# Attention and two routed expert layers on one core: score tiles paired 3 with 0 and 2 with 1, each in a PSUM bank of its own, and three pieces of work moved to other places of the head loop

## The chip, the cores and the metric

The kernel is one program on one core of a Trainium2 chip. The metric is the device time of one execution in microseconds (us). Below, PE is TensorE (PEld its weight loads), DVE is VectorE, ACT is ScalarE, POOL is GpSimd and SP the engine whose queue issues most DMAs.

## The reference

```python
# attention: 4 batches, 12 heads, 448 tokens, head size 64, causal
scores = scale * np.matmul(q, k.transpose(0, 1, 3, 2))
scores = np.where(mask, -1000000000.0, scores)
attn = np.exp(scores - np.max(scores, axis=-1, keepdims=True))
attn = attn / (np.sum(attn, axis=-1, keepdims=True) + 1e-09)
attn_out = np.matmul(attn, v)
x = attn_out.transpose(0, 2, 1, 3).reshape(1792, 768)
# two expert layers, each: every token goes to one of 8 experts
...
    h = np.maximum(x[mask] @ w1[e], 0.0)
    out[mask] = gate_w[mask, None] * (h @ w2[e])
```

The first expert layer adds its result to x and skips tokens whose skip score is not positive; the second uses normalised inner products with expert embeddings as router logits. All arrays are float32.

## The kernel before, in words

The program has two parts. The first, which the change touches, computes attention head by head and, along the way, the logits of both routers. The second part gathers the tokens of each expert and runs the expert layers; nothing of it is changed.

The first part is one loop over 48 heads (`for i in range(n)`, one turn of it is called a **step** here), whose instructions stand in each engine's queue in the order in which the Python code records them. Each engine works its queue off in order, and semaphores hold an instruction until what it needs is done. In step i the kernel does, for head i-1, the **scores** (`scores`, L307): four PE products, one for each block row c of 112 queries, with (c+1)*112 keys, so tiles of 112, 224, 336 and 448 columns for c = 0, 1, 2, 3. The head size is 64, so a product uses only 64 of the array's 128 rows; q and k lie in both halves of the partitions, and two tiles on different halves run at the same time. Then, on DVE, the **stage** (`stage_a`, L318) of each tile adds the mask, scales, and takes the row's extreme, and ACT takes the exponentials (L321). For head i-2 the step also **turns** the 10 blocks of probabilities by PE transposes into three tiles `tp` (`turn`, L331) and copies them out (two copies on DVE, one on ACT, L333).

Work for a pair of heads alternates between even and odd steps. In an **even** step PE multiplies the turned probabilities with the values (`stage_v`, 16 records at L342 into the tile `av`), makes the router products of an earlier pair (`router_pair`, L386, into columns of the tile `bank`; DVE adds them up in `ls`, L391), and ACT copies `av` to `xb` (L347). In an **odd** step PE turns `xb` back (`turn_v`, L353, tile `tv`), DVE divides by the sums and writes the attention output x (`norm_v`, three instructions, L359 to L361), and PE turns the new 128 columns of x for the router (`router_turn`, L373, tile `rt`), which ACT copies to `xs` (L376). `put_x` sends x to DRAM by DMAs from SP.

PSUM has eight banks. Before the change they hold: `s3` (score tile 3), `s20` (score tiles 2 and 0 together), `bank` (score tile 1, the router products `lt` and the logits), `av`, and four banks that are handed round under the tag `tp`. Tiles 2 and 0 use rows 64 to 127 of the array, tiles 3 and 1 rows 0 to 63.

When the logits of a batch are complete, a list of small jobs (`route`) is worked off, one a step: the logits of all tokens (L396 on PE), the choice of expert, the rank of a token within its expert (L460 to L465 on PE, then a chain of small DVE instructions that ends with L168), one-hot tables on POOL, and the entry into the token table (L525 on PE, L528 on DVE). This happens for three batches within the loop; the last batch is done behind it.

Of the kernel before, what the change touches and what calls it, by code (L numbers as in the profile page):

```python
# [7 lines left out]
F32 = mybir.dt.float32  # L8
# [10 lines left out]
B, H, S, D = 4, 12, 448, 64  # L19
CP = 112  # L20
NCH = S // CP
DM = H * D
DF = 1024
NE = 8
NTOK = B * S
P = 128
KC = DM // P
FC = DF // P
CT = 14
NCOL = CT * NE  # L30
# [5 lines left out]
NLG = 17  # L36
# [9 lines left out]
def moe_attention_kernel(tc, qk, vv, w_r, emb, tau, w11, w12, w21, w22, out):  # L46
# [25 lines left out]
    with ExitStack() as top:  # L72
# [148 lines left out]
        with ExitStack() as ctx:  # L221
            ld = ctx.enter_context(tc.tile_pool(name="ld", bufs=2))
            wk = ctx.enter_context(tc.tile_pool(name="wk", bufs=2))
# [32 lines left out]
            ern, en = inv_norm(sm, ess, NE, "en")  # L256

            def embed_squares():
                esq = wk.tile([NE, DM], F32, tag="pt", name="esq")
                nc.scalar.activation(esq, es, AF.Square, accum_out=ess)  # L260

            def embed():
                pe = ps.tile([P, 4 * CP], F32, tag="tp", name="pe", bufs=4)
                for k in range(KC):
                    nc.tensor.transpose(
                        pe[:, k * 8 : k * 8 + 8], es[:, k * P : (k + 1) * P], ident[:NE, :NE])
                nc.vector.tensor_copy(wr[:, :, 8:16], pe[:, 0:48].rearrange("p (k e) -> p k e", e=8))
# [8 lines left out]
                    small.pop(0)()  # L276


            bank = ps.tile([P, 4 * P], F32, tag="s1", name="bank")
            lt, lg_room = bank[:, 2 * CP : 3 * CP], bank[:CP, 3 * CP : 3 * CP + NCH * NLG]  # L280

            def busy_here(n):
                if n:
# [10 lines left out]
            def score_tiles():  # L294
                return dict(
                    st=wk.tile([CP, 10 * CP], F32, tag="st", name="st"),
                    mn=wk.tile([CP, NCH], F32, tag="mn", name="mn"),
                    pr=wk.tile([CP, 10 * CP], F32, tag="pr", name="pr"),
                    s3=ps.tile([CP, S], F32, tag="s3", name="s3"),
                    s20=ps.tile([CP, S], F32, tag="s20", name="s20"),  # L300
                    s1=bank[:CP, 0 : 2 * CP])

            def scores(src, a, c):

                n, r = (c + 1) * CP, 64 * (1 - c % 2)
                a[c] = (a["s20"][:, 3 * CP :], a["s1"], a["s20"][:, 0 : 3 * CP], a["s3"])[c]
                nc.tensor.matmul(a[c], src[r : r + 64, c * CP : (c + 1) * CP], src[r : r + 64, S : S + n],  # L307
                                 start=True, stop=True)

# [14 lines left out]
            def turn_p(pr, pt, i):  # L324

                nb = 4 if i < 2 else 2
                tp = ps.tile([CP, 4 * CP], F32, tag="tp", name="tp", bufs=4)
                for u in range(nb):
                    c, j = BLOCKS[4 * i + u]
                    o = (OFF[c] + j) * CP  # L330
                    nc.tensor.transpose(tp[:, u * CP : (u + 1) * CP], pr[:, o : o + CP], ident[:CP, :CP])  # L331
                dst = pt[:, 4 * i * CP : (4 * i + nb) * CP]
                (nc.scalar.copy if i == 1 else nc.vector.tensor_copy)(dst, tp[:, : nb * CP])  # L333

            def stage_v(g):

                b, hp = divmod(g, H // 2)
                av = ps.tile([P, S], F32, tag="av", name="av")
                for j in range(NCH):
                    o = BLOCKS.index((j, j)) * CP  # L340
                    for u in range(2):
                        nc.tensor.matmul(av[u * D : (u + 1) * D, j * CP :], v_t[b][:, j, 2 * hp + u, :],  # L342
                                         pts[2 * g + u][:, o : o + (NCH - j) * CP],
                                         start=(j == 0), stop=(j == NCH - 1))
                del pts[2 * g], pts[2 * g + 1]
                xb = wk.tile([P, S], F32, tag="xb", name="xb", bufs=1)
                return lambda: nc.scalar.copy(xb, av), xb  # L347

            def turn_v(xb):

                tv = ps.tile([CP, NCH, P], F32, tag="tp", name="tv", bufs=4)
                for t in range(NCH):
                    nc.tensor.transpose(tv[:, t, :], xb[:, t * CP : (t + 1) * CP], ident)  # L353
                return tv

            def norm_v(g, tv):
                b, hp = divmod(g, H // 2)
                rs = sums.pop(g)
                nc.vector.tensor_scalar(rs, rs, 1e-9, None, op0=ALU.add)  # L359
                nc.vector.reciprocal(rs, rs)  # L360
                nc.vector.tensor_tensor(  # L361
                    x_t[b][:, :, hp * P : (hp + 1) * P].rearrange("p t (u d) -> p t u d", u=2),
                    tv.rearrange("p t (u d) -> p t u d", u=2),
                    rs.unsqueeze(3).to_broadcast([CP, NCH, 2, D]), op=ALU.mult)
# [2 lines left out]

                return b == B - 1 and k == KC - 1

            def router_turn(b, k):  # L370
                rt = ps.tile([P, 4 * CP], F32, tag="tp", name="rt", bufs=4)
                for t in range(NCH):
                    nc.tensor.transpose(  # L373
                        rt[:, t * CP : (t + 1) * CP], x_t[b][:, t, k * P : (k + 1) * P], ident[:CP, :CP])
                xs = wk.tile([P, S], F32, tag="xs", name="xs")
                return lambda: nc.scalar.copy(xs, rt), (b, k, xs)  # L376
# [24 lines left out]
            def route(b):  # L401
# [3 lines left out]
                k = {"fill": []}  # L405
# [47 lines left out]

                def rank():
                    oh, some = k["oh"], k["some"]
                    rk = ps.tile([P, 4 * CP], F32, tag="tp", name="rk", bufs=4)
                    wd = NCH * 16
                    o16 = oh.rearrange("p t m e -> p t (m e)")
                    r16 = run[:CP].rearrange("p m e -> p (m e)")
# [60 lines left out]

                def enter(m):
                    roh, voh = k["made"][m]
                    tk = ps.tile([P, NCOL], F32, tag="tp", name="tk", bufs=4)
                    for t in range(NCH):
                        nc.tensor.matmul(tk, roh[:, t, :], voh[:, t, :], start=(t == 0), stop=(t == NCH - 1))  # L525
                    if fast:
                        first_index(0, tk)
                    nc.vector.tensor_tensor(tok[m], tok[m], tk, op=ALU.add)  # L528
                    while k["fill"]:
                        fill()  # L530
# [17 lines left out]
                        lambda: both(enters[0], q1), q2, q3, enters[1]]  # L548

            def turn(i):  # L550
                pts[i] = wk.tile([CP, 10 * CP], F32, tag="pt", name="pt")
                for u in range(3):
                    turn_p(prs[i], pts[i], u)

# [18 lines left out]
            spl, prs, pts, sums = {}, {}, {}, {}  # L573
            with tc.manual_schedule():
                busy_here(12)
                exps = []
                for i in range(n):
                    b, h = heads[i]
                    if h == 0:
# [12 lines left out]
                    if i in EARLY:  # L592
                        early_low(EARLY[i])
                    even = i % 2 == 0
                    if not even and i >= 5:
                        norm_v(i // 2 - 2, turn_v(xb))
                        put_x(i // 2 - 2)
                    if i >= 1:
                        sc = score_tiles()
                        prs[i - 1] = sc["pr"]  # L600
                        for c in (2, 3, 1, 0):
                            scores(spl[i - 1], sc, c)
                        exps = [stage_a(i - 1, sc, c) for c in (2, 3, 1)]
                        exps.pop(0)()
                        little()
                    little()
                    ended = None
                    if even and i >= 4:
                        copy_v, xb = stage_v(i // 2 - 2)
                    add = None  # L610
                    if even and i >= 6:
                        add = router_pair(*pair)
                        ended = pair[0] if pair[1] == KC - 1 else None
                    while exps:
                        exps.pop(0)()
                    if even and i >= 4:
                        copy_v()
                    if i >= 1:
                        stage_a(i - 1, sc, 0)()
                        little()  # L620
                    if add is not None:
                        add()
                    if i == 0:
                        embed_squares()
                    little()
# [2 lines left out]
                    if i >= 2:  # L628
                        turn(i - 2)
                    little()  # L630
                    if not even and i >= 5:
                        copy_x, pair = router_turn(*divmod(i // 2 - 2, H // 2))
                        copy_x()
                    if i == 3:
                        embed()
                    if i + 1 in EARLY:
# [3 lines left out]
                    if ended is not None:  # L640
                        later.extend(route(ended))

                sc = score_tiles()
                prs[n - 1] = sc["pr"]
                for c in (2, 3, 1, 0):
# [7 lines left out]
                    exps.pop(0)()  # L653
                add()
                turn(n - 2)
                norm_v(n // 2 - 2, turn_v(xb))
                later.pop(0)()
                turn(n - 1)
                copy_x, pair = router_turn(B - 1, KC - 2)
                later.pop(0)()  # L660
                copy_x()
                copy_v, xb = stage_v(n // 2 - 1)
# [544 lines left out]
```

## Time and profile before

| | us |
|---|---|
| median of 3 runs | 903.12 (901.76 to 904.38) |
| the profiled execution, its own time | 902.78 |
| its span, first to last instruction | 901.1 |
| PE busy | 824.0 (91%) |
| DVE busy | 554.4 (62%) |
| ACT busy | 474.8 (53%) |
| POOL busy | 135.2 (15%) |

The span is what the profiler shows; the execution's own time is 1.7 us longer. Busy times are sums over the whole program, and its two parts have different limits: the first part takes about the first 230 us of the span.

### The profile page before, as it was taken

What the parts mean: (1) busy time and instruction counts of PE and PEld (TensorE: products, weight loads), DVE (VectorE), ACT (ScalarE), POOL (GpSimd) and SP (SyncE); (2) the same over time, 40 slices, a digit from 0 to 9 for tenths busy, and PEclk for the clock granted to TensorE, in tenths of its full rate; (3) what the DMA queues carried; (4) which work ended last, traced back from release to release, by engine and by line L of the source; (5) the groups of instructions that cost most, each with busy time, mean ns of one, the idle gap of its engine ahead of it and who ended that gap; (6) DMA issues with size and microseconds to landing.
All of it is one profiled execution on the core that took longest, in us unless ns stands there. A gap on an engine that the chain in (4) does not pass through costs nothing. (4 is left out here: it accounts for less than half of the span.)

```text
span 901.1 us, 14898 instructions
## 1 busy us (share of the span) xinstructions
PE 824.0 (91%) x4960; PEld 686.5 (76%) x4960; DVE 554.4 (62%) x1641; ACT 474.8 (53%) x1013; POOL 135.2 (15%) x150
## 2 busy tenths in 40 slices
PE   7998989989797899899999879899999998999994
PEld 5665766666487788788899748789889887889884
DVE  5767767776566688378833476665283268574343
ACT  5777666666455466166612336454272256463252
POOL 1132404013201111011010021011111011110100
PEclk9999999999899899999999999999999999999998
DMA  8979565563636487267710354580451086361000
GB/s 243 315 271 299 165 185 165 167 206 139 202 140 258 175 300 286 72 232 300 299 45 28 145 198 159 197 332 21 149 211 51 19 313 267 133 238 41 37 1 18
DMA packets 59032, 158.22 MB, mean 176 GB/s; under 512 B 13013, under 2 KB 23765, under 8 KB 58448
## 3 DMA queue, kind: packets, MB, share of 16 engines
q1 hardware_dynamic: 52816, 139.33, 43.4%
q0 software_dynamic: 6080, 17.29, 5.4%
q8 instruction: 59, 0.97, 0.5%
q14 instruction: 77, 0.63, 0.2%
HBM read 146.45 MB, written 22.92 MB: 188 GB/s over the span
## 5 line engine op out<-in xcount | busy, mean ns | idle before, releaser
L789 PE MATMUL p<-hi,ht 128*128 128x384 f32 x960 | 241.8, 353 | 8.5 <-DVE ht L773 4.6
L740 DVE TENSOR_TENSOR lo<-raw,hi 128x768 fp32r<-128x768 f32 (+1 forms) x218 | 220.6, 1062 | 8.0 <-ACT hi L736 4.5
L781 PE MATMUL p<-hi,xt 128*128 128x512 f32 x720 | 183.3, 403 | 8.0 <-PEq L1088 3.3
L736 ACT CAST hi<-raw 128x768 fp32r<-128x768 f32 (+1 forms) x218 | 187.3, 923 | 0.6 <-DMA raw<-in_w 0.6
L789 PEld LDWEIGHTS p<-hi,ht 128*128 128x128 f32 x960 | 167.8, 191 | 14.7 <-DVE ht L773 10.6
L781 PEld LDWEIGHTS p<-hi,xt 128*128 128x128 f32 x720 | 140.4, 198 | 37.4 <-ACTq L1088 5.1
L321 ACT ACTIVATE pr<-st,mn 112x336 f32<-112x336 f32 x192 | 99.5, 520 | 60.4 <-DVE mn L318 60.4
L789 PE MATMUL p<-lo,ht 128*128 128x384 f32 x480 | 124.3, 340 | 0.4 <-issue 0.4
L773 DVE SCALAR_TENSOR_TENSOR ht<-tp,ht 128x512 fp32r<-128x512 f32 x60 | 41.4, 689 | 115.3 <-ACT ht L772 106.6
L781 PE MATMUL p<-lo,xt 128*128 128x512 f32 x360 | 96.2, 402 | 0.0
L940 ACT COPY hs<-p 128x512 f32<-128x512 f32 x60 | 34.8, 580 | 106.0 <-PE p L781 67.0
L789 PEld LDWEIGHTS p<-lo,ht 128*128 128x128 f32 x480 | 88.7, 191 | 0.5 <-issue 0.5
L760 ACT CAST xt<-tp 128x384 fp32r<-128x384 f32 (+2 forms) x62 | 30.4, 492 | 109.5 <-PE tp L754 108.8
L761 DVE TENSOR_TENSOR xt<-tp,xt 128x384 fp32r<-128x384 f32 (+2 forms) x62 | 33.3, 544 | 84.5 <-ACT xt L760 81.6
L318 DVE CUSTOM_DVE_ANT_0 st<-s,mask 112x336 f32<-112x336 f32 x144 | 63.5, 465 | 29.4 <-PE s L307 17.8
L781 PEld LDWEIGHTS p<-lo,xt 128*128 128x128 f32 x360 | 67.8, 195 | 11.4
L772 ACT ACTIVATE ht<-tp 128x512 fp32r<-128x512 f32 x60 | 36.0, 600 | 55.1 <-PE tp L798 49.4
L331 PE MATMUL tp<-ident,pr 112*112 112x112 f32 x480 | 57.3, 267 | 0.0
L307 PE MATMUL s<-qk 64*112 64x112 f32 (+2 forms) x288 | 49.6, 450 | 7.1 <-DVE mn L318 7.1
L331 PEld LDWEIGHTS tp<-ident,pr 112*112 112x112 f32 x480 | 47.1, 136 | 8.6 <-issue 7.8
L818 POOL DMA_INDIRECT out<-py,pidx x18 | 19.7, 1093 | 207.7 <-ACT hi L736 75.5
L342 PE MATMUL av<-pt,v 112*64 112x448 f32 (+3 forms) x384 | 50.6, 405 | 0.0
(201 smaller groups left out, 908.3 us busy)
## 6 DMA issues: line engine op xcount, KB each, us to landing
raw<-in_w SPq DMA_DIRECT2D x96, 512.0 KB
raw<-in_w SPq DMA_DIRECT2D x128, 384.0 KB
qk<-in_qk SPq DMA_DIRECT2D x23, 896.0 KB
x<-x SPq DMA_DIRECT2D x24, 448.0 KB
v<-in_vv SPq DMA_DIRECT2D x4, 1344.0 KB
qk<-in_qk SPq DMA_DIRECT2D x2, 448.0 KB
g_n<-x,L POOLq DMA_INDIRECT x23, 4.4
out<-py,pidx POOLq DMA_INDIRECT x18, 3.4
```

What stands on the lines that cost most here:

```text
L307: nc.tensor.matmul(a[c], src[r : r + 64, c * CP : (c + 1) * CP], src[r : r + 64, S : S + n], start=True, stop=True)
L318: nc.vector.tensor_tensor_reduce(out=so, in0=a[c], in1=mask[:, S - n : S], scale=-0.125, scalar=3.0e38, op0=ALU.add, op1=ALU.min, accum_ou ...
L321: return lambda: nc.scalar.activation(a["pr"][:, OFF[c] * CP : OFF[c] * CP + n], so, AF.Exp, bias=mn, scale=-1.0, accum_out=rs)
L331: nc.tensor.transpose(tp[:, u * CP : (u + 1) * CP], pr[:, o : o + CP], ident[:CP, :CP])
L342: nc.tensor.matmul(av[u * D : (u + 1) * D, j * CP :], v_t[b][:, j, 2 * hp + u, :], pts[2 * g + u][:, o : o + (NCH - j) * CP], start=(j == ...
L736: copy(hi, raw)
L740: eng.tensor_tensor(lo, raw, hi.bitcast(F32), op=ALU.subtract)
L772: nc.scalar.activation(hi, src, AF.Relu)
L773: nc.vector.scalar_tensor_tensor(lo, src, 0.0, hi.bitcast(F32), op0=ALU.max, op1=ALU.subtract)
L781: nc.tensor.matmul(p1[u], xt[:, k, :, j], r[:, u * 512 : (u + 1) * 512], start=(k == 0 and j == 0 and not low), stop=(k == KC - 1 and low))
L789: mm = nc.tensor.matmul(p2[u], l, r[:, u * (DM // 2) : (u + 1) * (DM // 2)], start=(f == 0 and j == 0), stop=(f == FC - 1 and j == len(ter ...
L940: nc.scalar.copy(hs[:, u * 512 : (u + 1) * 512], p1[u])
```

## The change

The four score tiles get a bank each. Tile 0 moves into `bank`, beside `lt` and the logits; tiles 1, 2 and 3 have tiles of their own. Tiles 3 and 0 use array rows 0 to 63, tiles 2 and 1 rows 64 to 127. The stages of all four tiles are now recorded together. `tp` has three banks in place of four. `av`, `tv` and `rt` share one bank under the tag `av`. In an even step `router_turn` (of the pair before) moves to the head of the step, ahead of the scores, and `router_pair` and then `stage_v` to its end, behind the turn of head i-2. In an odd step the copy of `av` and the addition to `ls` stand first, then the scores and the four stages, and then `turn_v` and `norm_v`, which stood ahead of the scores before. The turned probabilities `pt` have three buffers in place of two. Behind the loop, the last steps follow the same order and use the tag `tp` where the change gives one.

```diff
             def scores(src, a, c):
-                n, r = (c + 1) * CP, 64 * (1 - c % 2)
-                a[c] = (a["s20"][:, 3 * CP :], a["s1"], a["s20"][:, 0 : 3 * CP], a["s3"])[c]
+                n, r = (c + 1) * CP, (0, 64, 64, 0)[c]
+                a[c] = (a["s0"], a["s1"], a["s2"], a["s3"])[c]
...
-                av = ps.tile([P, S], F32, tag="av", name="av")
+                av = turned_room("av")[:, 0:S]
...
+            def turned_room(tag):
+                return ps.tile([P, 4 * P], F32, tag=tag, name="turned", bufs=3 if tag == "tp" else 1)
...
-                    if not even and i >= 5:
-                        norm_v(i // 2 - 2, turn_v(xb))
-                        put_x(i // 2 - 2)
+                    if even and i >= 6:
+                        copy_x, pair = router_turn(*divmod(i // 2 - 3, H // 2))
+                        copy_x()
+                    if not even and i >= 5:
+                        copy_v()
+                        if add is not None:
+                            add()
                     if i >= 1:
...
-                        exps = [stage_a(i - 1, sc, c) for c in (2, 3, 1)]
-                        exps.pop(0)()
+                        exps = [stage_a(i - 1, sc, c) for c in (2, 3, 1, 0)]
                         little()
                     little()
-                    ended = None
-                    if even and i >= 4:
-                        copy_v, xb = stage_v(i // 2 - 2)
-                    add = None
-                    if even and i >= 6:
-                        add = router_pair(*pair)
-                        ended = pair[0] if pair[1] == KC - 1 else None
+                    if not even and i >= 5:
+                        norm_v(i // 2 - 2, turn_v(xb))
+                        put_x(i // 2 - 2)
                     while exps:
                         exps.pop(0)()
-                    if even and i >= 4:
-                        copy_v()
                     if i >= 1:
-                        stage_a(i - 1, sc, 0)()
                         little()
-                    if add is not None:
-                        add()
...
                     if i >= 2:
                         turn(i - 2)
                     little()
-                    if not even and i >= 5:
-                        copy_x, pair = router_turn(*divmod(i // 2 - 2, H // 2))
-                        copy_x()
+                    ended, add = None, None
+                    if even and i >= 6:
+                        add = router_pair(*pair)
+                        ended = pair[0] if pair[1] == KC - 1 else None
+                    if even and i >= 4:
+                        copy_v, xb = stage_v(i // 2 - 2)
```

What stands in the queues shows the moves better. The first place is PE in an odd step and the head of the even step behind it; `s_` with a number is a score tile, `turned` the shared bank. Before:

```order
L353 MATMUL tv<-ident,xb 112x128 x4
L307 MATMUL s_499<-qk_330 112x336
L307 MATMUL s_498<-qk_330 112x448
L307 MATMUL bank<-qk_330 112x224
L307 MATMUL s_499<-qk_330 112x112
L331 MATMUL tp<-ident,pr 112x112 x10
L373 MATMUL rt<-ident,x_123 128x112 x4
L307 MATMUL s_546<-qk_330 112x336
```

and with the change:

```order
L308 MATMUL s_495<-qk_333 112x336
L308 MATMUL s_494<-qk_333 112x448
L308 MATMUL s_496<-qk_333 112x224
L308 MATMUL bank<-qk_333 112x112
L358 MATMUL turned<-ident,xb 112x128 x4
L332 MATMUL tp<-ident,pr 112x112 x10
L378 MATMUL turned<-ident,x_123 128x112 x4
L308 MATMUL s_553<-qk_333 112x336
```

The transposes of `xb` (L353, now L358) moved behind the scores of their step; those for the router (L373, now L378) still stand between the odd step's turn and the even step's scores, but they now turn the columns of x which the odd step itself has just made.

The second place is DVE in the same odd step, with the semaphores that each instruction waits for; ISA is the stage of a score tile. Before:

```order
L359 TENSOR_SCALAR rs<-rs 112x8
L360 RECIPROCAL rs<-rs 112x8 [waits DVE_49]
L361 TENSOR_TENSOR x_123<-tv,rs 112x4x128 [waits DVE_49,PE_49]
L318 ISA st,mn<-s_605,mask 112x336 [waits PE_49,Activation_49]
L318 ISA mn 112x1
L318 ISA st,mn<-s_604,mask 112x448
...
L318 ISA st,mn<-bank,mask 112x224
...
L318 ISA st,mn<-s_605,mask 112x112
...
L333 COPY pt<-tp 112x448 [waits PE_49,Activation_49]
```

and with the change:

```order
L319 ISA st,mn<-s_605,mask 112x336 [waits PE_49,Activation_49]
L319 ISA mn 112x1
L319 ISA st,mn<-s_604,mask 112x448 [waits PE_49]
...
L319 ISA st,mn<-s_606,mask 112x224 [waits PE_49]
...
L319 ISA st,mn<-bank,mask 112x112 [waits PE_49]
...
L364 TENSOR_SCALAR rs<-rs 112x8
L365 RECIPROCAL rs<-rs 112x8 [waits DVE_49]
L366 TENSOR_TENSOR x_123<-turned,rs 112x4x128 [waits DVE_49,PE_49]
L334 COPY pt<-tp 112x448 [waits PE_49]
```

The three instructions of `norm_v` moved from ahead of the four stages to behind them. Before, only the first stage waits for PE; with the change each stage has a wait of its own.

The third place is PE in an even step, behind its scores. Before:

```order
L342 MATMUL av<-pt,v_121 64x448 x2
...
L342 MATMUL av<-pt,v_121 64x112 x2
L386 MATMUL bank<-xs,wr 32x112 x4
L331 MATMUL tp<-ident,pr 112x112 x10
L353 MATMUL tv<-ident,xb 112x128 x4
```

and with the change:

```order
L332 MATMUL tp<-ident,pr 112x112 x10
L391 MATMUL bank<-xs,wr 32x112 x4
L343 MATMUL turned<-pt,v_121 64x448 x2
...
L343 MATMUL turned<-pt,v_121 64x112 x2
```

The turn moved ahead, and the router's products and then the values' products come last; the router's products write the tile `bank`, in which score tile 0 of the same step now lies. The order of SP's DMAs is the same in both kernels.

## Rows read from the trace of the kernel before

**Rows 1.** Busy time by stretch: length, busy us (instructions) by engine, PE clock, DMA share, GB/s:

```profile
21.45:215.38 193.94, 179.98 (x1488) 126.94 (x1488) 141.82 (x585) 135.26 (x433) 45.59 (x54) 0.98 0.68 221
```

**Rows 2.** Timeline of PE, odd and even step: start, us, line, operation (idle in brackets):

```profile
203.81 1.01 PE L307 MATMUL s<-qk 64*112 64x336 f32 x6
204.66 0.54 PE L307 MATMUL bank<-qk 64*112 64x224 f32 x2
205.13 1.17 PE L331 MATMUL tp<-ident,pr 112*112 112x112 f32 x10
206.14 0.55 PE L373 MATMUL rt<-ident,x 112*128 112x112 f32 x4
206.99 1.01 PE L307 MATMUL s<-qk 64*112 64x336 f32 x6 [0.30 <-DVE mn L318]
...
208.31 2.11 PE L342 MATMUL av<-pt,v 112*64 112x448 f32 x16
210.34 0.40 PE L386 MATMUL bank<-xs,wr 128*32 128x112 f32 x8
210.67 1.17 PE L331 MATMUL tp<-ident,pr 112*112 112x112 f32 x10
211.68 0.60 PE L353 MATMUL tv<-ident,xb 128*112 128x128 f32 x4
212.21 0.63 PE L307 MATMUL s<-qk 64*112 64x336 f32 x2
```

**Rows 3.** Timeline of PE, narrow windows: through tile 2's last pass; tile 1's first pass:

```profile
206.99 0.81 PE L307 MATMUL s<-qk 64*112 64x336 f32 x3 [0.30 <-DVE mn L318]
...
207.84 0.35 PE L307 MATMUL bank<-qk 64*112 64x224 f32 x1
```

**Rows 4.** Timeline of DVE in the odd step of rows 2:

```profile
203.81 0.16 DVE L359 TENSOR_SCALAR rs<-rs 112x8 f32<-112x8 f32 x1
...
204.30 0.69 DVE L361 TENSOR_TENSOR x<-tv,rs 112x512 f32<-112x512 f32 x1
205.37 0.51 DVE L318 CUSTOM_DVE_ANT_0 st<-s,mask 112x336 f32<-112x336 f32 x1 [0.37 <-PE s L307]
...
206.85 0.08 DVE L318 DVE_READ_ACCUMULATOR2_ANT mn<- 112x1 f32 x1
206.85 0.92 DVE L333 COPY pt<-tp 112x448 f32<-112x448 f32 x2
```

**Rows 5.** Timeline of ACT in the same step:

```profile
205.92 0.57 ACT L321 ACTIVATE pr<-st,mn 112x336 f32<-112x336 f32 x1 [2.04 <-DVE mn L318]
...
207.98 0.51 ACT L333 COPY pt<-tp 112x448 f32<-112x448 f32 x1
```

**Rows 6.** Timeline of PE and DVE in two steps with router jobs:

```profile
76.74 0.41 PE L396 MATMUL bank<-ident,ls 128*112 128x68 f32 x2 [1.59 <-DVE mn L318]
76.99 1.12 PE L331 MATMUL tp<-ident,pr 112*112 112x112 f32 x10
...
87.98 0.16 DVE L484 TENSOR_SCALAR base<-bm 112x8 f32<-112x8 f32 x1
...
88.84 0.16 DVE L168 TENSOR_TENSOR lp_o<-base,lp_c 112x8 f32<-112x8 f32 x1
```

**Rows 7.** Timeline of PE in the first steps:

```profile
9.10 1.01 PE L307 MATMUL s<-qk 64*112 64x336 f32 x6 [2.04 <-DVE mn L318]
...
15.95 0.50 PE L265 MATMUL pe<-ident,x 8*128 8x8 f32 x6 [1.05 <-issue]
```

**Rows 8.** PE's waits by line, 21.45 to 215.38 us: total, times, longest:

```profile
PE bank L396 <- DVE mn L318: 4.8, 3, 1.6
...
PE rt L373 <- DVE rks L476: 2.7, 3, 0.9
```

**Rows 9.** Busy time in two stretches of that part; the clock is third from the end:

```profile
131.40:134.80 3.40, 3.40 (x16) 2.74 (x15) 1.92 (x9) 1.57 (x6) 0.00 (x0) 0.50 0.21 60
186.00:189.40 3.40, 3.40 (x18) 3.12 (x20) 1.92 (x11) 2.00 (x8) 0.00 (x0) 0.50 0.02 5
```

More of the change, by code (lines that the diff above doesn't have):

```diff
@@ L258, in embed_squares @@
             def embed_squares():
-                esq = wk.tile([NE, DM], F32, tag="pt", name="esq")
+                esq = wk.tile([NE, DM], F32, tag="pt", name="esq", bufs=3)
                 nc.scalar.activation(esq, es, AF.Square, accum_out=ess)
             def embed():
-                pe = ps.tile([P, 4 * CP], F32, tag="tp", name="pe", bufs=4)
+                pe = ps.tile([P, 4 * CP], F32, tag="tp", name="pe", bufs=3)
                 for k in range(KC):
@@ L276, in little @@
                     small.pop(0)()
-            bank = ps.tile([P, 4 * P], F32, tag="s1", name="bank")
-            lt, lg_room = bank[:, 2 * CP : 3 * CP], bank[:CP, 3 * CP : 3 * CP + NCH * NLG]
+            bank = ps.tile([P, 4 * P], F32, tag="s0", name="bank")
+            lt, lg_room = bank[:, CP : 2 * CP], bank[:CP, 2 * CP : 2 * CP + NCH * NLG]
             def busy_here(n):
@@ L299, in score_tiles @@
                     s3=ps.tile([CP, S], F32, tag="s3", name="s3"),
-                    s20=ps.tile([CP, S], F32, tag="s20", name="s20"),
-                    s1=bank[:CP, 0 : 2 * CP])
+                    s2=ps.tile([CP, 3 * CP], F32, tag="s2", name="s2"),
+                    s1=ps.tile([CP, 2 * CP], F32, tag="s1", name="s1"),
+                    s0=bank[:CP, 0:CP])
             def scores(src, a, c):
-                n, r = (c + 1) * CP, 64 * (1 - c % 2)
-                a[c] = (a["s20"][:, 3 * CP :], a["s1"], a["s20"][:, 0 : 3 * CP], a["s3"])[c]
+                n, r = (c + 1) * CP, (0, 64, 64, 0)[c]
+                a[c] = (a["s0"], a["s1"], a["s2"], a["s3"])[c]
                 nc.tensor.matmul(a[c], src[r : r + 64, c * CP : (c + 1) * CP], src[r : r + 64, S : S + n],
@@ L326, in turn_p @@
                 nb = 4 if i < 2 else 2
-                tp = ps.tile([CP, 4 * CP], F32, tag="tp", name="tp", bufs=4)
+                tp = ps.tile([CP, 4 * CP], F32, tag="tp", name="tp", bufs=3)
                 for u in range(nb):
@@ L347, in stage_v, with turn_v @@
                 return lambda: nc.scalar.copy(xb, av), xb
-            def turn_v(xb):
-                tv = ps.tile([CP, NCH, P], F32, tag="tp", name="tv", bufs=4)
+            def turned_room(tag):
+                return ps.tile([P, 4 * P], F32, tag=tag, name="turned", bufs=3 if tag == "tp" else 1)
+            def turn_v(xb, tag="av"):
+                tv = turned_room(tag)[:CP].rearrange("p (t n) -> p t n", t=NCH)
                 for t in range(NCH):
@@ L368, in direct, with router_turn @@
                 return b == B - 1 and k == KC - 1
-            def router_turn(b, k):
-                rt = ps.tile([P, 4 * CP], F32, tag="tp", name="rt", bufs=4)
+            def router_turn(b, k, tag="av"):
+                rt = turned_room(tag)[:, 0 : 4 * CP]
                 for t in range(NCH):
@@ L455, in rank @@
                     oh, some = k["oh"], k["some"]
-                    rk = ps.tile([P, 4 * CP], F32, tag="tp", name="rk", bufs=4)
+                    rk = ps.tile([P, 4 * CP], F32, tag="tp", name="rk", bufs=3)
                     wd = NCH * 16
@@ L522, in enter @@
                     roh, voh = k["made"][m]
-                    tk = ps.tile([P, NCOL], F32, tag="tp", name="tk", bufs=4)
+                    tk = ps.tile([P, NCOL], F32, tag="tp", name="tk", bufs=3)
                     for t in range(NCH):
@@ L550, in turn @@
             def turn(i):
-                pts[i] = wk.tile([CP, 10 * CP], F32, tag="pt", name="pt")
+                pts[i] = wk.tile([CP, 10 * CP], F32, tag="pt", name="pt", bufs=3)
                 for u in range(3):
@@ L575, in moe_attention_kernel @@
                 busy_here(12)
-                exps = []
+                exps, add = [], None
                 for i in range(n):
@@ L641, in moe_attention_kernel @@
                         later.extend(route(ended))
+                copy_x, pair = router_turn(B - 1, KC - 3, "tp")
+                copy_x()
                 sc = score_tiles()
@@ L655, in moe_attention_kernel @@
                 turn(n - 2)
-                norm_v(n // 2 - 2, turn_v(xb))
+                norm_v(n // 2 - 2, turn_v(xb, "tp"))
                 later.pop(0)()
                 turn(n - 1)
-                copy_x, pair = router_turn(B - 1, KC - 2)
+                copy_x, pair = router_turn(B - 1, KC - 2, "tp")
                 later.pop(0)()
```

## The prediction

> **What bounds the kernel now.** I read the busy time by stretch first, then the timelines of PE, DVE and ACT over one pair of steps, then PE's list of waits. Between 21.45 and 215.38 us lies the loop from step 5 to the scores of the last head: 21 pairs of an odd and an even step, and step 47. PE is busy there for 179.98 of 193.94 us, DVE for 141.82 [rows 1]. So PE looks like the bound, but that is an average over two kinds of step.
>
> An ordinary pair lasts 8.40 us (203.81 to 212.21) [rows 2]. The even step, 206.99 to 212.21, is 5.22 us and PE does not wait in it: scores 1.32, values 2.03, router products 0.33, turn 1.01, transposes of `xb` 0.53. The odd step is 3.18 us and ends with a wait: PE stands 0.30 before the next scores until DVE has read the last score tile. Its length is DVE's: from the start of the scores 1.56 us until the first stage starts (203.81 to 205.37), 1.56 for the four stages (205.37 to the end of the last read at 206.93), 0.06 until PE goes on [rows 2, 4]. `norm_v` costs nothing now: DVE runs it (203.81 to 204.99) while PE still makes the scores.
>
> **The change, part by part.**
>
> *Halves of the rows.* Before, one half of the array carries 448 + 224 columns, the other 336 + 112; with the change both carry 560. The longer half loses 112 columns. The second pass over tile 1's 224 columns adds 0.54 - 0.35 = 0.19 us [rows 2, 3], so two passes of 112 are 0.19, and the block falls from 1.32 to 1.13. That is 0.19 in each step, if PE is what the step waits for.
>
> *A bank and a signal for each tile.* The first stage now waits for tile 2 alone. Tile 2's last pass ends 0.81 after the scores start [rows 3]; before, the first stage started 0.17 after the end of the last product (204.66 + 0.54 = 205.20, to 205.37) [rows 2, 4]. So it starts at 0.98 in place of 1.56, 0.58 earlier. Lower bound 0.90, if a single wait is quicker; upper bound 1.56, if DVE in effect still waits for all four, against which stands that each stage has its own wait. Tile 3 follows without a gap: all passes of the `s` tiles are over 1.01 after the start, 0.2 behind tile 2 [rows 2, 3], and tile 2's stage lasts 0.51 [rows 4]. I take 0.98.
>
> *Odd step.* Now the order on DVE is four stages, then `norm_v`; and the router's transposes at the next head need the x which this `norm_v` writes. The chain is: first stage at 0.98; the instruction behind the stages starts 1.48 later (205.37 to 206.85); `norm_v` takes 1.18 (203.81 to 204.99); PE goes on 0.06 later, at 3.70 [rows 4]. PE itself is ready earlier: scores 1.13, transposes of `xb` 0.53, turn 1.01, so at 2.67. **A new wait of 1.03 us**, ahead of the transposes for the router; behind it in PE's queue stand the next head's scores, so everything waits. The transposes take 0.55 (0.85 to the next scores, less the 0.30) [rows 2]. The odd step is 3.70 + 0.55 = 4.25, against 3.18.
>
> *Even step.* Scores 1.13 and turn 1.01: PE reaches the router's products at 2.14. They write `bank`, where tile 0 of the same step lies, and must wait for its stage: 0.98 + 1.56 + 0.06 = 2.60. A second wait, 0.46. Then router products 0.33 and values 2.03: 4.96, against 5.22. Why a wait is due between different columns of one tile shows in the row on the logits: they too lie in `bank` beside a score tile, and PE stood 1.59 us there until DVE had read it [rows 6]. The Trainium skill, "PSUM — Partial Sum Buffer", section "PSUM bank collisions raise a hardware error", wants PSUM guarded by bank and not by address; the row agrees. By addresses alone the even step would be 0.46 shorter.
>
> *Sum for a pair:* 4.25 + 4.96 = **9.21 against 8.40**. The 0.19 of the halves is in neither chain: both go from the start of the scores to tile 2 and then through DVE. The Trainium skill, "TensorEngine Tiling (Array Packing)", section "PSUM Bottleneck", warns that tiling speeds up TensorE and not the emptying of PSUM; that speaks against this edit, and rows 4 agree, with 1.56 us of stages behind a block of 1.32.
>
> *What is hidden.* The copy of `av` (0.51, ACT, like its copy in [rows 5]) at the odd step's head runs during the scores; without that cover it would add 0.5. Exponentials start 0.55 after the first stage and their copy ends 2.57 after they start [rows 4, 5], so at about 4.1 in the odd step; the next turn comes at 4.25 + 1.13. The two copies of `pt` (0.92) and the addition to `ls` follow on DVE during the wait-free values' products. The third `pt` buffer and three `tp` banks in place of four cost nothing in an ordinary pair, since a turn uses three. `put_x`'s DMAs issue some 2.5 us later in the step; behind them on SP stand the next q, k and weights, which are needed steps later.
>
> *Router jobs.* They make some steps of a batch longer in both kernels. With the change, per batch: the logits wait for tile 0's stage until 2.60, cost 0.25 [rows 6], and the turn of 1.01 ends at 3.86 against 3.70: +0.16. The choice of expert is about 1 us of small DVE work behind the copies, which delays the next first stage by about 0.2. In the rank step the third `tp` waits for ACT's copy at 4.1: +0.65; the chain behind it, 1.02 (87.98 to 89.00) [rows 6], delays the next first stage by 0.3. The two entries into the token table hold the third `tp` until DVE has added: +0.4 each. Together 2.1 a batch; of the third batch only the first 1.3 fall in this part: 5.5.
>
> *Sum.* 21 x 9.21 + 4.25 + 5.5 = 203.2, against 193.94: **+9.2**. *First steps:* the second head's scores no longer wait 2.04 [rows 7], since tile 2's bank is free after its own stage; the turn behind it is then set by the exponentials, 1.1 earlier; the embeddings' wait of 1.05 shrinks a little, and step 4 has no `xb` to turn: together I estimate -2.3 (between -3.5 and -0.5). *Last steps:* three `tp` banks for more users, +0.5 (0 to 1.5). *Clock:* PE ran at half its clock, 1.2 in place of 2.4 GHz, for two stretches of 3.4 us, each soon after a wait of 1.59 [rows 6, 8, 9]; a third such wait and all of 0.9 had none. A stretch at half costs at most half its length, about 1.6. The waits of 1.59 are gone, those of 1.03 are many, one a batch is about 1.4. The 193.94 holds two such stretches, my 203.2 holds none; I add one, +1.6 (0 to 5).
>
> 9.2 - 2.3 + 0.5 + 1.6 = +9.0. The profiled execution took 902.78, 1.7 more than its span; that gives 911.8. The median of the runs is 0.34 above it: **912 us**. The second part is unchanged and starts later by as much.
>
> **The rivals.**
>
> *Faster, because the router's transposes do not wait.* If x were ready when PE has turned, the odd step would end at 2.67 + 0.55 and the pair be 8.18: 22 x 1.03 less, 889 us. If the even step's wait went too, 879. For it: DVE is idle for over a quarter of the part [rows 1]. Against it: the four stages and `norm_v` are one after the other on one engine, with measured lengths. It decides when a pair comes out 0.4 shorter than 9.21, 0.2 in each step's way through DVE.
>
> *No difference.* A pair near 8.8, which the start of the first stage at 0.90 and shorter latencies would nearly give, or a larger gain at the beginning: 901 to 905.
>
> *Slower still by the clock.* PE now idles 1.5 us in every pair. Should some six more stretches run at half, the time is about 922; ten, 928. For it: two waits of 1.59 were followed by such a stretch [rows 6, 9]. Against it: waits of 0.9 were not. The Trainium skill, "TensorE: Matmul & The Clock Gate", section "HAM oscillation — how this bites in real kernels", tells of kernels that lose clock through idle spells between groups of products; no ordinary pair shows it here.
>
> *Slower still by the signals.* If the first stage still starts at 1.56, both steps are 0.58 longer: 21 x 1.16 more, 936.
>
> **How the numbers follow.** My forecast has 0.72, with 907 to 918 as its own range (0.1 a pair either way is 2 us, the beginning and the clock the rest). The clock has 0.10, the signals 0.03, no difference 0.07, faster 0.08. About 0.3% (2.7 us) is what a measurement of this kernel can tell from no change. Slower is thus 0.85, the same 0.07, faster 0.08. The range that leaves out no more than 2 in 10 is 904 to 921.
>
> **What would show it.** Right: PE idle about 1 us ahead of the router's transposes in nearly every even step, released by DVE's instruction that writes x; about 0.45 ahead of the router's products, released by the read of `mn`; a pair of 9.2 us; first stages about 1.0 after the scores start; a score block of 1.13. Wrong: transposes for the router without a wait, first stages at 1.5, a pair under 8.6, or granted clock well under 0.98 in this part.

## The result and the profile after

The changed kernel takes 915.02 us (median of 4 runs, 913.47 to 917.46), the kernel before 903.15 in the same comparison (901.76 to 904.38): ratio 1.0136, 95% interval 1.0114 to 1.0158. The forecast was 912, range 904 to 921, slower. The profiled execution took 914.93, its span is 913.2. The top of its page:

```profile
span 913.2 us, 14795 instructions
PE 819.6 (90%) x4960; PEld 685.6 (75%) x4960; DVE 550.3 (60%) x1641; ACT 476.7 (52%) x1013; POOL 138.3 (15%) x150
```

Busy time by stretch: the first steps, the stretch from step 5 to the last head's scores that answers to [rows 1], and the one half-clock stretch ahead of it (length, busy us by engine, PE clock third from the end):

```profile
4.80:22.62 17.82, 12.89 (x86) 9.38 (x85) 12.05 (x60) 10.76 (x37) 0.00 (x0) 0.90 0.88 242
22.62:226.58 203.96, 172.54 (x1493) 125.79 (x1492) 138.21 (x587) 139.19 (x439) 45.64 (x54) 1.00 0.66 208
17.40:20.80 3.40, 3.40 (x19) 2.69 (x17) 2.47 (x10) 2.39 (x9) 0.00 (x0) 0.50 0.49 154
```

The loop is 10.02 us longer than in [rows 1] although PE is busy 7.44 less: PE waits more. The first steps end 1.17 later (22.62 against 21.45). What follows the last head's scores takes 913.2 - 226.58 = 686.6 against 901.1 - 215.38 = 685.7. So 10.0 of the 12.1 us of span lie in the loop. PE's list of waits there (us in total, times, longest) names two new ones:

```profile
PE turned L378 <- DVE x L366: 12.9, 13, 1.3
PE bank L391 <- DVE mn L319: 6.3, 16, 0.6
```

Together they are 19.2 of the 31.4 us for which PE is idle in the loop; before, it was idle there for 14.0.

The timeline of PE over an ordinary pair (odd step from 212.61, even step from 216.87) answers to [rows 2]:

```profile
212.61 1.19 PE L308 MATMUL s<-qk 64*112 64x336 f32 x6
213.46 0.35 PE L308 MATMUL bank<-qk 64*112 64x112 f32 x2
213.75 0.65 PE L358 MATMUL turned<-ident,xb 128*112 128x128 f32 x4
214.23 1.12 PE L332 MATMUL tp<-ident,pr 112*112 112x112 f32 x10
216.33 0.60 PE L378 MATMUL turned<-ident,x 112*128 112x112 f32 x4 [0.98 <-DVE x L366]
216.87 1.19 PE L308 MATMUL s<-qk 64*112 64x336 f32 x6
...
218.00 1.17 PE L332 MATMUL tp<-ident,pr 112*112 112x112 f32 x10
219.54 0.40 PE L391 MATMUL bank<-xs,wr 128*32 128x112 f32 x8 [0.37 <-DVE mn L319]
219.87 2.11 PE L343 MATMUL turned<-pt,v 112*64 112x448 f32 x16
221.91 0.63 PE L308 MATMUL s<-qk 64*112 64x336 f32 x2
```

The pair is 9.30 long (most are 4.24 + 5.04 = 9.28), 8.40 before. Its two brackets are the two new waits: 0.98 ahead of the router's transposes, ended by the instruction of `norm_v` that writes x, and 0.37 ahead of the router's products, ended by the read of `mn` behind tile 0's stage. DVE in the same pair answers to [rows 4]:

```profile
213.58 0.51 DVE L319 CUSTOM_DVE_ANT_0 st<-s,mask 112x336 f32<-112x336 f32 x1 [2.47 <-PE s L308]
...
215.06 0.20 DVE L364 TENSOR_SCALAR rs<-rs 112x8 f32<-112x8 f32 x1
215.29 0.20 DVE L365 RECIPROCAL rs<-rs 112x8 f32<-112x8 f32 x1
215.59 0.69 DVE L366 TENSOR_TENSOR x<-turned,rs 112x512 f32<-112x512 f32 x1
216.19 0.91 DVE L334 COPY pt<-tp 112x448 f32<-112x448 f32 x2
217.83 0.51 DVE L319 CUSTOM_DVE_ANT_0 st<-s,mask 112x336 f32<-112x336 f32 x1 [0.73 <-PE s L308]
...
219.31 0.08 DVE L319 DVE_READ_ACCUMULATOR2_ANT mn<- 112x1 f32 x1
```

DVE stands idle for 2.47 us until tile 2 is there, works through the stages and `norm_v` with pauses of 0.1 at most, and PE waits for the end of just that chain. Neither engine is full; each waits for the other in turn.

By its ordinary pairs the loop would have lost more: 21 times 0.88 and 1.06 for the last odd step are 19.5. Steps with the router's jobs gave 9.5 of that back: over and above ordinary steps they and the two half-clock stretches [rows 9] took 14.4 before and 4.8 with the change, where the jobs fall into time in which PE waits anyway.

PE in the first steps answers to [rows 7]:

```profile
6.68 1.55 PE L308 MATMUL s<-qk 64*112 64x336 f32 x6 [0.48 <-DVE mn L319]
...
12.21 1.17 PE L308 MATMUL s<-qk 64*112 64x336 f32 x6 [2.10 <-DMA qk<-in_qk]
...
16.31 0.53 PE L265 MATMUL pe<-ident,x 8*128 8x8 f32 x6 [1.80 <-ACT pt L334]
...
18.37 2.11 PE L332 MATMUL tp<-ident,pr 112*112 112x112 f32 x10
```

The last line lies in the half-clock stretch: ten transposes take 2.11 there, 1.12 to 1.17 in the pair above.

### The profile page after: what moved, and what is told of

Read it like the earlier page. It is cut to its first block, busy times and chain, and to the rows that moved or that the text cites. A ratio compares the mean times of both kernels' runs of the same rounds, so it can differ in the third digit from the quotient of the medians.

```text
span 913.2 us, 14795 instructions
## 1 busy us (share of the span) xinstructions
PE 819.6 (90%) x4960; PEld 685.6 (75%) x4960; DVE 550.3 (60%) x1641; ACT 476.7 (52%) x1013; POOL 138.3 (15%) x150
## 5 line engine op out<-in xcount | busy, mean ns | idle before, releaser
L785 PE MATMUL p<-hi,xt 128*128 128x512 f32 x720 | 184.0, 404 | 10.5 <-PEq L1092 3.9
L319 DVE CUSTOM_DVE_ANT_0 st<-s,mask 112x336 f32<-112x336 f32 x144 | 65.5, 504 | 66.8 <-PE s L308 66.0
L308 PE MATMUL s<-qk 64*112 64x448 f32 (+2 forms) x288 | 58.1, 476 | 2.6 <-DMA qk<-in_qk 2.1
L343 PE MATMUL turned<-pt,v 112*64 112x448 f32 (+3 forms) x384 | 50.7, 406 | 0.0
```

The costliest lines, as they stand in the source:

```text
L319: nc.vector.tensor_tensor_reduce(out=so, in0=a[c], in1=mask[:, S - n : S], scale=-0.125, scalar=3.0e38, op0=ALU.add, op1=ALU.min, accum_ou ...
L785: nc.tensor.matmul(p1[u], xt[:, k, :, j], r[:, u * 512 : (u + 1) * 512], start=(k == 0 and j == 0 and not low), stop=(k == KC - 1 and low))
```

## The experiments

The theory under test was the prediction's: an ordinary pair pays for two waits of PE on DVE's chain, one made by the place of the router's transposes, one by the place of the router's products. Rivals were a loss by the clock, a loss by the new tiles and banks themselves, and a gain from the halves that something else eats. All kernels compute the same as the kernel before; no work is left out.

**1. Router's transposes behind the scores** (place alone; everything else as changed):

```diff
-                    if even and i >= 6:
-                        copy_x, pair = router_turn(*divmod(i // 2 - 3, H // 2))
-                        copy_x()
...
                         for c in (2, 3, 1, 0):
                             scores(spl[i - 1], sc, c)
+                        if even and i >= 6:
+                            copy_x, pair = router_turn(*divmod(i // 2 - 3, H // 2))
+                            copy_x()
```

> Theory (two waits in a row of PE behind DVE): with the router's transposes behind the even step's scores, x is written (3.7 us after the odd step's scores began) before PE comes to them, so the wait of 1.0 us ahead of them goes. The wait ahead of the router's products stays or grows, since DVE, still busy with the odd step, now begins the even step's stages late (about 4.5 us after the odd step's scores began): a pair of about 8.5 in place of 9.28, about 899 us. Rival (the time went with the shared bank of the turned tiles and the third tp bank, not with the order): both stay, so 913 to 917.

Measured: 902.26 (10 runs), ratio 1.0008 (0.9985 to 1.003), 3 above the 899 expected. The odd step falls from 4.24 to 2.67, the pair to 8.46. PE's list of waits over the loop (total, times, longest) shows where part of the gain stays:

```profile
PE bank L391 <- DVE mn L319: 6.3, 10, 0.8
...
PE bank L391 <- ACT pr L322: 3.6, 5, 0.7
```

Of the wait for x at L378 one of 0.2 is left, and the one ahead of the router's products has grown. DVE comes late to the even step: in the pair at 201.61 it is still at the odd step's copies when the even step's scores start (204.28), the first stage starts 1.74 later (0.96 in the changed kernel), and PE waits 0.75 for the read of tile 0.

**2. Values ahead of the router's products** at the end of the even step:

```diff
                     ended, add = None, None
+                    if even and i >= 4:
+                        copy_v, xb = stage_v(i // 2 - 2)
                     if even and i >= 6:
                         add = router_pair(*pair)
                         ended = pair[0] if pair[1] == KC - 1 else None
-                    if even and i >= 4:
-                        copy_v, xb = stage_v(i // 2 - 2)
```

> Theory: with the values' products ahead of the router's products, tile 0's stage is over before PE comes to the tile bank, and the wait of 0.4 to 0.5 us in each even step goes; the wait of the odd step stays. Pair about 8.77, about 904 us. Rival (only the wait at the router's transposes sets the pace, and what is saved here is waited for there): 913 to 917.

Measured: 903.66 (10 runs), ratio 1.0021 (1.0001 to 1.0042). The pair is 4.23 + 4.60 = 8.83. The wait ahead of the transposes stays, the other is covered by the values' products:

```profile
205.20 0.61 PE L378 MATMUL turned<-ident,x 112*128 112x112 f32 x4 [0.94 <-DVE x L366]
205.74 1.19 PE L308 MATMUL s<-qk 64*112 64x336 f32 x6
...
207.97 2.11 PE L343 MATMUL turned<-pt,v 112*64 112x448 f32 x16
210.01 0.40 PE L391 MATMUL bank<-xs,wr 128*32 128x112 f32 x8
```

**3. Both moves.**

> Both moves together. Theory: neither wait is left in an ordinary pair and PE's own products set it, 7.6 to 7.7 us; about 882 us, and in any case well under the kernel before. Rival (DVE's or ACT's load, not the place of the waits, keeps the pair from going under that of before): 900 or more.

Measured: 889.73 (4 runs, 885.75 to 897.01), ratio 0.9876 (0.9811 to 0.994): faster than the kernel before, but 8 above the 882 expected. The pair came out as foreseen, 2.67 + 4.99 = 7.66, as long as PE's work:

```profile
189.21 1.19 PE L308 MATMUL s<-qk 64*112 64x336 f32 x6
190.06 0.35 PE L308 MATMUL bank<-qk 64*112 64x112 f32 x2
190.34 0.65 PE L358 MATMUL turned<-ident,xb 128*112 128x128 f32 x4
190.83 1.12 PE L332 MATMUL tp<-ident,pr 112*112 112x112 f32 x10
191.88 1.19 PE L308 MATMUL s<-qk 64*112 64x336 f32 x6
...
193.01 0.60 PE L378 MATMUL turned<-ident,x 112*128 112x112 f32 x4
193.45 1.12 PE L332 MATMUL tp<-ident,pr 112*112 112x112 f32 x10
194.50 2.11 PE L343 MATMUL turned<-pt,v 112*64 112x448 f32 x16
196.54 0.40 PE L391 MATMUL bank<-xs,wr 128*32 128x112 f32 x8
196.87 1.20 PE L308 MATMUL s<-qk 64*112 64x336 f32 x6
```

No bracket is left. The loss of the change was thus made by two places in the queue, and not by its tiles and banks. What was not foreseen are the steps with the router's jobs: the loop takes 181.65 (19.89 to 201.54), 18.1 more than ordinary steps alone, where the changed kernel had 4.8. PE still waits 12.1 us in it, most of them at jobs, and these now lengthen the loop.

**4. The new tiles, halves and banks in the order of before** (shared bank for `av`, `tv`, `rt`; three `tp`, the four stages recorded together; the moves undone).

> The kernel before in its own order, with the change's score tiles, halves and banks (three tp banks, one bank for the three turned tiles), and the four stages recorded together. Theory (what an order costs is its waits, and the banks alone don't shorten the way round): the odd step is short, about 2.7, since the next scores wait only for tile 2's bank, but the values' products now wait about 1 us for ACT's copy of the router's transposes out of the shared bank; a pair of about 8.7 against 8.40, 905 to 912 us. Rival (the new halves and banks are a gain by themselves, and only the moves lose it): a pair of 7.7 to 8.0, under 895.

Measured: 893.0 (4 runs, 892.2 to 893.97), ratio 0.9889 (0.9855 to 0.9922): the expectation of 905 to 912 missed. The pair came out as foreseen, 2.62 + 6.0 = 8.62, with the wait that the shared bank makes:

```profile
205.81 2.11 PE L343 MATMUL turned<-pt,v 112*64 112x448 f32 x16 [0.87 <-ACT xs L377]
```

But the steps with router jobs were cheaper than worked out (even ones 5.04, without that wait), so from the first scores to the last head's the attention took 206.8 against 209.8. Some 2.0 of that was lost again between the loop and the expert layers. And the expert layers, whose code nothing here touches, took 650.4 from their first transposes to the end of the span, against 658.1. Experiments 9 to 11 ask why.

**5 and 6. The old halves** in the changed kernel, and in the kernel with both moves:

```diff
-                n, r = (c + 1) * CP, (0, 64, 64, 0)[c]
+                n, r = (c + 1) * CP, 64 * (1 - c % 2)
```

> The changed kernel with tiles 3 and 1 on one half of the rows and 2 and 0 on the other, as before; banks and order stay changed. Theory (the 0.19 us of a shorter score block lie in front of a wait, so they are worth nothing): 914 to 917, with the block at 1.32 and the waits shorter by 0.19 each. Rival (the halves pay in each of 48 steps): 924.

> The kernel with both moves (e3, pair 7.66) and the old halves, tiles 3 and 1 on one half. Theory (the halves pay where no wait stands behind the score block): both steps 0.19 longer, a pair of 8.04, about 8 us slower than e3, near 898. Rival (they pay nowhere, something else sets e3's pair): pair still 7.66, 890.

Measured in the changed kernel: 918.43 (912.38 to 920.84), ratio 1.0192 (1.0152 to 1.0233), a little above the 914 to 917 expected, and the times don't tell it from the change. The steps do: 4.23 + 5.04, the same, and the loop 203.99 for 203.96. PE's scores take longer and its waits are shorter by as much, 10.5 in 13 times ahead of L378 in place of 12.9. With both moves the same edit costs 0.19 in each step, 2.86 + 5.18 against 2.67 + 4.99, and 897.22 (8 runs, ratio 0.9946, 0.9923 to 0.997). The halves are worth what was counted for them, once no wait stands behind them.

**7 and 8. The embeddings' transposes in the shared bank** in place of the third `tp`, in the changed kernel and with both moves:

```diff
-                pe = ps.tile([P, 4 * CP], F32, tag="tp", name="pe", bufs=3)
+                pe = ps.tile([P, 4 * P], F32, tag="av", name="turned")
```

> The changed kernel with the embeddings' transposes in the bank of the turned tiles, which is free then, in place of a tp bank. Theory (of the 1.80 us wait in the first steps about 1.0 is for the third tp bank, the rest for the scaled embeddings): the wait falls to about 0.8 and is released by DVE's scaling. Rival (it waits for the embeddings anyway, as the kernel before did for 1.05): it stays above 1.5. The time of one run tells nothing at this size.

> Both moves and the embeddings' transposes in the turned tiles' bank: the candidate that should beat both kernels. Theory: e3's time less 0 to 2 us, 886 to 890, about 1.5% faster than before. Rival: no better than e3, or within 0.3% of before.

In the changed kernel (912.14, one run) the wait falls from 1.80 to 0.87 and is ended by another instruction:

```profile
14.80 0.53 PE L265 MATMUL turned<-ident,x 8*128 8x8 f32 x6 [0.87 <-DVE x L271]
```

With both moves it is 1.14, ended by the same instruction. What that is worth in time is not shown: step 5's scores start at 20.32 and 20.34, and at 19.89 to 22.62 in the five profiles of kernels with the first steps of the changed one (table below). With both moves the time is 891.35 (6 runs, ratio 0.9848, 0.9809 to 0.9888), not to be told from experiment 3, where 886 to 890 was expected.

**9 to 11. ACT's waits without a releaser.** In the expert layers of the kernel before, ACT stands twice for 5 to 6 us where the profile names nothing it waits for ("issue"):

```profile
278.79 0.58 ACT L940 COPY hs<-p 128x512 f32<-128x512 f32 x1 [5.91 <-issue]
...
304.63 0.48 ACT L835 COPY yt<-tp 128x384 f32<-128x384 f32 x1 [4.86 <-issue]
```

Ahead of the first, the instruction that waits for PE's product ended at 273.65; the copy behind it began at 278.79. PE waits for the second one (`pm` <- `yt`, 3.2 us), and a half-clock stretch of 6.8 us begins at 305.47. (A third such line, 4.1 us ahead of L835 at 521.22, is in every kernel; there the transposes that it copies began only at 520.59.) The changed kernel and experiments 1 to 3 and 5 to 8 have such a pair at another place of the program, the same one in all of them (424.27 and 449.55 in the changed kernel, 4.23 and 5.58). Experiment 4 has neither. The three groups differ in how many instructions the trace records on ACT: 1432, 1408 and 1454. The work is the same; the number of instructions that only wait for a semaphore differs. So small copies that nobody reads were added on ACT, which is idle for 30% of the loop [rows 1]:

```diff
+                    if 8 <= i < 30:
+                        nc.scalar.copy(dz, ident[:NE, 0:1])
```

This is one copy a step, 22 in all; for 46 it is two a step in steps 8 to 30. The ratios in the table are to the kernel before as measured beside each.

> The kernel before with 22 copies of 8 numbers on ACT, one a step in steps 8 to 29, that nobody reads; nothing else is changed. It asks where the 7.7 us come from that the kernel with the new tiles in the old order won behind the attention, where its code is that of before. In every kernel of this case but that one ACT stands twice for 4 to 6 us in the expert layers with nothing to wait for, at the same place in its program in all kernels with the same number of ACT instructions (at 278.79 and 304.63 us in the kernel before). Theory code: these waits are for ACT's own code and depend on how many instructions stand ahead of them; the 22 copies bring the kernel before to the count of the kernel with tiles alone, so both waits go and the time is about 894 (903 less 8 to 9, plus up to 1 for the copies). Theory timing: they hang on when the attention ends against the transfers of weights; 22 copies on an engine that is idle for a third of the attention move that by less than 1 us, so both waits stay and the time is 902 to 904.

> Both moves (values ahead of the router's products, router's transposes behind the scores) with 46 such copies on ACT, two a step in steps 8 to 30, which bring it too to the count of the kernel with tiles alone. Theory code: ACT's waits ahead of 398.06 and 423.26 us go, and the time falls from about 890 to about 881. Theory timing: both waits stay and the time is 889 to 892.

> The kernel before with 46 copies of 8 numbers on ACT, two a step in steps 8 to 30, that nobody reads. With 22, one a step, each copy had taken the place of one instruction on ACT that only waits for a semaphore, so that ACT's count of instructions stayed 1432 and both waits without a releaser stayed at their places. With two a step the second copy has no such instruction to take the place of, and the count grows by about 23, to about 1455. Theory code: both waits (ahead of 278.79 and 304.63 us in the kernel before) go, and the time falls from 902 or 903 to 893 to 896. Theory timing: both stay, and the time is 902 to 906.

| kernel | ACT instructions | the two waits of ACT | us, ratio |
|---|---|---|---|
| before | 1432 | 5.91, 4.86 | 903.15 |
| before, 22 copies | 1432 | 5.87, 4.70, same place | 901.71, 0.9976 (0.9942 to 1.001) |
| before, 46 copies | 1452 | none | 893.31, 0.9907 (0.988 to 0.9934) |
| both moves | 1408 | 4.14, 5.53, the other place | 889.73, 0.9876 |
| both moves, 46 copies | 1440 | none | 882.62, 0.9753 (0.9725 to 0.9781) |

The 22 copies each took the place of an instruction that only waits, so the count stayed and the waits stayed: the expected 894 missed, for a reason that speaks for the theory. With 46 the count rose and both waits went, in both kernels. The same place in the kernel before with 46 copies:

```profile
277.29 0.59 ACT L944 COPY hs<-p 128x512 f32<-128x512 f32 x1 [0.81 <-PE p L785]
...
297.65 0.86 ACT L839 COPY yt<-tp 128x384 f32<-128x384 f32 x2 [0.92 <-ACT hi L740]
```

In all 13 traces the place of these waits goes with the number of ACT's instructions and not with when the attention ends: in the eight kernels with 1408 the last head's scores start between 201.5 and 226.7 us, and the waits stand at the same place of the program. That ACT waits there for its own code is only argued: two 8 KB packets of the instruction queue fall into each of the four waits of the kernel before and of the changed one, and the DMA engines move weights at some 400 GB/s when they begin. The Trainium skill, "Runtime: NRT & Kernel Launch", section "Instruction fetch mechanics", says that an engine's code is fetched ahead in blocks and that crossing into a new block is mostly hidden; if these waits are such crossings, most of the 4.1 to 5.9 us of each was not. The kernel with both moves and 46 copies, 882.62, is the fastest here.

## Why the prediction was right, point by point

**The odd step, right.** 4.25 foreseen, 4.24 measured in ordinary steps. The first stage starts 0.97 after the scores (0.98 foreseen; 1.56 before), so the signals of single tiles work as argued, and the rival by which they don't is refuted. The wait ahead of the router's transposes is 0.98 for 1.03; experiments 1 and 3 take it away by its place alone. It stands in 13 of the 21 pairs, fewer than the "nearly every" of the forecast: in the other eight a wait of a router's job, of 0.8 to 1.3 us, ahead of the logits or for `tp`, stands in its place, and no odd step is shorter than 4.22.

**The even step, right, 0.08 short.** 4.96 foreseen, 5.04 measured. The wait between columns of one bank is there. What was mis-sized is PE's way back to work: 0.15 us from the end of the read (219.39) to the products (219.54), where 0.06 was taken from another wait of PE. An instruction that only waits for a semaphore stands ahead of these products (219.44) and none ahead of the router's transposes; that it costs the 0.09 is not shown.

**Loop.** 203.2 was summed, without a half-clock stretch; 203.96 was measured, and its clock is 1.00. 21 pairs of 9.28 and an odd step of 4.24 make 199.1, so the router's jobs cost 4.8 for 5.5; the even steps' 0.08 and the odd steps' -0.01 make the other 1.5.

**Halves, right.** They change no step of this order (experiment 5). The Trainium skill, "TensorEngine Tiling (Array Packing)", section "PSUM Bottleneck", by which packing the array does not speed up the emptying of PSUM, agrees: 0.00 with the waits on DVE, 0.19 a step without them.

**The first steps, mis-sized, and less certain than one profile shows.** They were to bring 2.3 and cost 1.2 in the two profiles compared. Eight profiles have the first steps of one or the other kernel, since their edits begin later:

| first steps as in | half clock in them, us | wait of the second head's scores | wait ahead of the embeddings | step 5's scores start |
|---|---|---|---|---|
| before | 0 | 2.04 | 1.05 | 21.45 |
| before (experiment 9) | 3.4 | 2.04 | 1.05 | 23.03 |
| before (experiment 11) | 10.2 | 2.04 | 1.05 | 25.14 |
| the change | 3.4 | 0.48 | 1.80 | 22.62 |
| the change (experiment 1) | 3.4 | 0.28 | 2.16 | 22.19 |
| the change (experiment 10) | 3.4 | 0.68 | 1.80 | 22.18 |
| the change (experiment 2) | 0 | 0.23 | 1.80 | 20.10 |
| the change (experiment 3) | 0 | 0.63 | 1.97 | 19.89 |

The step "the second head's scores no longer wait 2.04" held but for 0.23 to 0.68. The step that failed is "the embeddings' wait of 1.05 shrinks a little": it grew to 1.80 and more, for the third `tp`, which ACT still had to copy out. Experiment 7 bears that out: the wait halves when the transposes use another bank. The 2.10 for q and k that had not landed stands in this one profile of the five. Without a half-clock stretch the first steps end 1.4 to 1.6 earlier than before, a gain for 2.3 foreseen; with one of 3.4 us on both sides, 0.4 to 0.9. Of the 3.5 by which the beginning missed its forecast, 2.1 to 2.7 go with the half-clock stretch: so much later do the three profiles with one start step 5 than the two without, in the same first steps.

**The clock, right in number by luck, wrong in place.** One stretch was added in the sum, for the loop (as 1.6; half of 3.4 is 1.7). The loop has none, in spite of 31.4 us of idle time of PE; the one that came stands in the first steps, and other profiles of the same first steps have none. The rival by the clock is refuted for the loop.

**The last steps.** +0.5 foreseen, +0.9 measured, 0.4 of it in the expert layers.

So the loop's loss was 0.8 larger than summed, the last steps' 0.4, and the beginning worse by 3.5, less the 1.6 that the clock had been given: 915 in place of 912. The loop's 10 us are the mechanism that was forecast; that the clock's 1.6 paid for part of the beginning is luck.

## What to carry to other kernels

Before a piece of work is moved in an in-order queue, ask what it waits for at its new place and what stands behind it: transposes moved ahead of the next scores waited about 1 us in 13 of 21 pairs for a result that was due just then, and two places turned a change worth -1.2% into +1.4%. A saving on an engine pays only where no wait stands behind it: the halves gave 0.00 or 0.19 us a step. When code that nobody touched becomes faster or slower by 8 us, look for an engine that waits for nothing, and count its instructions, before you credit the edit.

## What the runs showed of the hardware

- ACT stood still for 4 to 6 us twice, at places that go with the number of instructions in its own program; 20 instructions more took 8.6 us off the kernel before (893.31 against 901.88 in that comparison).
- PE idle for 31.4 of 204 us, in pieces of at most 1.4, kept its full clock (granted clock 1.00). In the first steps, waits of 2.1 and 1.8 were followed by a stretch at half clock in the changed kernel, waits of 1.8 and 2.0 by none in experiments 2 and 3; what decides there stays open.
- PE went on 0.06 us after the instruction of DVE that it waited for in one place, and 0.15 in another.
- Products on different halves of the array's rows can start out of the queue's order: before the change the 112-column tile 0 (rows 64 to 127) started at 149.10, the 224-column tile 1 queued ahead of it (rows 0 to 63) at 149.29.
